# Attention and two mixture-of-experts layers on one core: a small copy moves from ScalarE to VectorE and two range checks move to other places

## The chip, the cores and the metric

The kernel runs on one core of a Trainium2 chip. The metric is the device time of that core in microseconds (us), and the figure compared is the median of the timed runs. The engines are named as the profile names them: PE is TensorE's matmul, PEld its weight load, DVE is VectorE, ACT is ScalarE, POOL is GpSimd, SP is SyncE. In the trace each engine works off its own list of instructions, one behind another, and where it stands idle the row names the engine that released it.

## What is computed

A recurrent attention over 768 steps for 4 batches of 8 heads of width 40, then a router that sends each of the 3072 tokens to one of 8 experts, then a second two-layer net. Cut to what matters here:

```python
def _attn_ref(r, k, v, w, a, b):
    state = np.zeros((B, H, D, D)); y = np.zeros_like(r)
    for t in range(S):
        y[:, :, t] = einsum('bhd,bhde->bhe', rt, state)
        Sa = einsum('bhde,bhe->bhd', state, at)
        state = state * wt[:, :, None, :] - einsum('bhd,bhe->bhde', Sa, bt)
        state = state + einsum('bhd,bhe->bhde', vt, kt)

def reference(...):
    x = attention reshaped to (3072, 320)
    x = moe(x)      # argmax gate, relu(x @ w1[e]) @ w2[e], times the gate
    return moe2(x)  # (max(h,0) + alpha*min(h,0)) @ w_out with h = x @ w_in
```

## The kernel before

The attention handles the time axis in chunks of 64 steps. Its 3072 rows are cut into six groups (two pairs of batches by three stretches of 256 steps); in this document they are group 1 to group 6, in the code `os[0]` to `os[5]`. A group has four chunks for each of two batches, so eight slots, 48 slots in all. A chunk is solved in closed form: the decay products of its steps come from scans, the chunk's triangular matrix is inverted, and what is left is matmuls.

What a group needs before its slots:

- `prepare` (lines 440 to 477), four times a group: three loads, a range check of the decays on ACT (line 466), the backward scan `s` on DVE (467), a reciprocal on DVE (468), the forward scan `q` on DVE (469), two multiplications into `kb` on POOL (472), the copy of the scan's first column into `o.s0` on ACT (473), two multiplications into `abd` on POOL (476).
- `products` (479 to 506) and `sides` (508 to 523), eight times: matmuls into `lp`, copies of the triangular part `l1`, `l2` by ACT (497, 498), one fill of `l2` by POOL (503), the masked product `la` by DVE (504), and transposes whose results ACT evacuates (517, 523).
- `inverse` (528 to 613), once: `ul`, a block transpose of `l2` by DVE (535); then 31 steps of two DVE instructions each that build `ut` (553, 555), with `tmp` and pieces of `ul` in a one-buffer PSUM bank of tag `mg`; then two block transposes of `ut` by DVE, `ttc` (575) and `t11` (578, called `t` in the profile); four POOL copies for each half that put the diagonal blocks into `tt` (571); and for each half a matmul `zp`, ACT copies `z` (603), a matmul `yp`, ACT copies back into `tt` (612). The `zp` of the first half lies in the same `mg` bank as `tmp`.

Two checks of the inverse stand in its second half (589, 590). `check` (431 to 436) squares and sums its source on ACT; it writes the squares to a place that it may spoil, and the sum to one column of `checks`. The check of `ut` spoils `ut` itself, so it has to come after the last reader of `ut`, the transpose `t11`. The check of `l1` spoils `ttc`, so it has to come after the eight POOL copies that read `ttc`. In the timelines of ACT the instructions listed behind a check start only after it.

In the main loop (854 to 884) each slot runs `stage_a` to `stage_e`; DVE's part in a slot is `va` (696), the state update `yc` and `sm` (711, 712) and `rs` (724), POOL's part is `vg` (675), `va` (665), `yt` (725) and, each second slot, two indirect DMAs for the router (971). The inverse of a group is asked for at the first slot of the group before it, and its second half at the first slot of its own.

Only the first prologue is written out by hand as a schedule. After that a scheduler (`schedule_with_timeline_sim=True`) chooses the order on each engine when the program is built, by a timeline of its own, with `issue_after` as a further constraint. So an edit can change the order of instructions that it does not name. The first group (`o.start`) is handled in the prologue and keeps its checks as they are.

Of the kernel before, what the change touches and what calls it, by code (L numbers as in the profile page):

```python
# [9 lines left out]
F32 = mybir.dt.float32  # L10
# [4 lines left out]
AF = mybir.ActivationFunctionType  # L15
# [5 lines left out]
P = 128  # L21
# [269 lines left out]
class Attention:  # L291
# [9 lines left out]
    def __init__(self, tc, ctx, k, wP, kbP, aP, rvP, vrow, rt):  # L301
        nc = self.nc = tc.nc
        self.tc = tc
        self.k = k
        self.wP, self.kbP, self.aP, self.rvP, self.vrow = wP, kbP, aP, rvP, vrow
        st = ctx.enter_context(tc.tile_pool(name="at_st", bufs=1))
        self.early = ExitStack()
        self.pa = self.early.enter_context(tc.tile_pool(name="at_a", bufs=1, side="right"))
        self.p = ctx.enter_context(tc.tile_pool(name="at", bufs=2))
        self.ctx = ctx  # L310
        self.ps = ctx.enter_context(tc.tile_pool(name="at_ps", bufs=1, space=PSUM))
        self.ut_room = ExitStack()
        self.pools = {"ut": self.ut_room.enter_context(tc.tile_pool(name="at_ut", bufs=1, space=PSUM))}
        self.count = {}
        self.region = ExitStack()
        self.region.enter_context(tc.manual_schedule(engines={mybir.EngineType.DVE, mybir.EngineType.Pool, mybir.EngineType.Activation}))

        self.st = st
        V, G = nc.vector, nc.gpsimd
        every = lambda t: t  # L320
        nw = 2 * NCS * CW
        zero = st.tile([P, 1], F32, name="zero")
        nc.vector.memset(zero, 0.0)
        def clear(t):

            nc.scalar.copy(t, zero[:t.shape[0]].to_broadcast(list(t.shape)))

        self.clear = clear
        ring = self.ring
        self.wz = ring("wz", 2, [PP, nw + 1], None, pool=self.pa)  # L330
        self.kb = ring("kb", 2, [P, 2 * NCS, 2, C], None, pool=self.pa)
        self.abd = ring("abd", 2, [P, 2 * NCS, P], None, pool=self.pa)
        V.memset(self.wz[0], 0.9)
        for eng, t in ((V, self.kb[0]), (G, self.kb[1]), (G, self.abd[0]), (G, self.abd[1])):
            eng.memset(t, 0.0)
        self.d1s = ring("d1s", 1, [PP, nw], V, (every, 1e-10), (lambda t: t.rearrange("p (c t) -> p c t", t=CW)[:, :, C:], 1.0), dt=BF16, pool=self.pa)[0]
        self.z = ring("z", 1, [P, 2, 8, C], G, (every, 0.0), pool=self.pa)[0]
        self.d1q = ring("d1q", 1, [PP, nw], V, (every, 0.0), pool=self.pa)[0]
        V.memset(self.wz[1], 0.9)
        self.ra = ring("ra", 2, [PP, 2 * NCS, C], None, pool=self.pa)  # L340
        self.tt = ring("tt", 3, [P, 2, 8, P], None)
        flat = lambda t: t.rearrange("p a b c -> p (a b c)")
        for t in self.tt[:2]:
            self.clear(flat(t))

        self.kb_start = self.kb + [self.tt[0][:, i].rearrange("p u (x t) -> p u x t", x=2) for i in range(2)]
        self.abd_start = self.abd + [self.tt[1][:, i] for i in range(2)]
        self.mid = ring("mid", 1, [P, 1], G, (every, -0.9 * 1.24))[0]
        self.checks = ring("checks", 1, [P, 36], G, (every, 0.0))[0]

        self.negmask = ring("negmask", 1, [P, C], G, (every, -1.0))[0]
        self.posmask = ring("posmask", 1, [P, C], G, (every, 1.0))[0]
        for q in range(2):
            r = slice(q * 64, q * 64 + 64)
            for t, sg in ((self.negmask, 1), (self.posmask, -1)):
                nc.gpsimd.affine_select(t[r], t[r], pattern=[[-sg, C]], compare_op=ALU.is_gt, fill=0.0, base=0, channel_multiplier=sg)
        self.ncheck = 0
        self.rt = rt
# [13 lines left out]
    def ring(self, name, n, shape, eng, *fills, dt=F32, pool=None):  # L372
        pool = pool or self.st
        out = []
        for i in range(n):
            t = pool.tile(shape, dt, name=f"{name}{i}", bufs=1)
            for sel, val in fills:
                eng.memset(sel(t), val)
            out.append(t)
        return out  # L380
# [59 lines left out]
    def prepare(self, o, pg):  # L440

        nc = self.nc
        nw = 2 * NCS * CW
        half, bb = divmod(pg, 2)
        p4 = slice(4 * bb, 4 * bb + 4)
        if pg == 0:
            o.s0 = self.p.tile([PP, 8, NCS], F32, name="s0", bufs=4)
            o.group, o.q, o.la, o.kbr = {}, {}, {}, {}
        if bb == 0:
            o.q[half] = self.p.tile([PP, 8, 2, CW], F32, name="q", bufs=5)  # L450
        kbs, abds = (self.kb_start, self.abd_start) if o.start else (self.kb, self.abd)
        wz, ra, kb, abd = (self.ringed(*n) for n in (("wz", self.wz), ("ra", self.ra), ("kb", kbs), ("abd", abds)))
        for q in range(2):
            r = slice(q * HQ, q * HQ + D)
            nc.sync.dma_start(wz[r], self.wP[o.bp, o.g, pg, q])
            nc.sync.dma_start(kb[r].rearrange("p a x t -> p (a x t)"), self.kbP[o.bp, o.g, pg, q])
            nc.sync.dma_start(ra[r].rearrange("p a t -> p (a t)"), self.aP[o.bp, o.g, pg, q])
        w3 = wz[:, :nw].rearrange("p (c t) -> p c t", t=CW)[:, :, 1:]
        s = self.pa.tile([PP, nw], F32, name="s", bufs=2)
        s3 = s.rearrange("p (c t) -> p c t", t=CW)  # L460
        qt = o.q[half][:, p4]
        qc = qt.rearrange("p a c t -> p (a c) t")
        if o.start:
            self.check(w3, self.pa.tile([P, 2 * NCS, C], F32, name="junk", tag="t4", bufs=3)[:PP], 1.24, self.mid)
        else:
            self.check(w3, qc[:, :, :C], 1.24, self.mid)
        nc.vector.tensor_tensor_scan(s[:, ::-1], wz[:, 1:][:, ::-1], self.d1s[:, ::-1], 0.0, ALU.mult, ALU.max)  # L467
        nc.vector.reciprocal(self.d1q.rearrange("p (c t) -> p c t", t=CW)[:, :, 0], s3[:, :, 0])
        nc.vector.tensor_tensor_scan(qt.rearrange("p a c t -> p (a c t)"), wz[:, :nw], self.d1q, 0.0, ALU.mult, ALU.max)  # L469
        for x in range(2):  # L470
            eng = nc.vector if o.start else nc.gpsimd
            eng.tensor_tensor(kb[:PP, :, x, :], kb[:PP, :, x, :], s3[:, :, 1:], op=ALU.mult)
        nc.scalar.copy(o.s0[:, p4, 2 * half:2 * half + 2], s3[:, :, 0].rearrange("p (a c) -> p a c", c=2))
        for q in range(2):
            r = slice(q * HQ, q * HQ + D)
            nc.gpsimd.tensor_tensor(abd[r, :, q * C:(q + 1) * C], ra[r], qc[r, :, :C], op=ALU.mult)  # L476
        o.group[pg] = abd.rearrange("p (a c) t -> p a c t", c=2), kb.rearrange("p (a c) x t -> p a c (x t)", c=2)
# [50 lines left out]
    def inverse(self, o):  # L528

        nc = self.nc  # L530
# [31 lines left out]
        def vacant(half):  # L562
            if not o.start:
                for lo, hi in zip(lows, highs):
                    nc.gpsimd.memset(o.tt[half][lo, :, :, hi], 0.0)

        def diagonal(half):
            for q in (1, 3, 0, 2):
                r = slice(32 * q, 32 * q + 32)
                eng = nc.vector if o.start and half == 0 else nc.gpsimd  # L570
                eng.tensor_scalar(o.tt[half][r, :, :, 32 * q:32 * q + 32], ttc[r, 2 * half:2 * half + 2], 1.0, 0.0, op0=ALU.mult, op1=ALU.add)

        vacant(0)
        ttc = self.t4("ttc")
        nc.vector.transpose(ttc.rearrange("p c u t -> p t (c u)"), ut)
# [9 lines left out]
        for half in range(2):  # L585
            if half:
                vacant(1)
                diagonal(1)
                self.check(ut, ut, 0.01)
                self.check(l1.rearrange("p c u j -> p (c u) j"), ttc.rearrange("p c u t -> p (c u) t"), 0.01)  # L590
                yield
            tt = o.tt[half]
            zp = self.work("zp", [P, 8, C], "mg" if o.start or half == 0 else "w1")
# [15 lines left out]
                nc.tensor.matmul(yp[c2 * 64:c2 * 64 + w.shape[1], u], lhsT=w, rhs=z[:, c2, u, :], start=True, stop=True)  # L609
            for c2 in range(2):  # L610
                for q, (lo, hi) in enumerate(zip(lows, highs)):
                    nc.scalar.activation(tt[lo, c2, :, hi], out(yp, c2, q), AF.Copy, scale=-1.0)
            yield


# [120 lines left out]
    def run(self, rt, sp, moe, ctx):  # L736
        tc, nc = self.tc, self.nc
        os = []
        for bp in range(B // 2):
            for g in range(S // SL):  # L740
                o = K()
                o.bp, o.g, o.rv, o.start = bp, g, {}, not os
                os.append(o)
        per = 2 * NCS
        n_slots = per * len(os)
# [144 lines left out]
    def bad(self, okm):  # L890

        nc = self.nc
        assert self.ncheck == 36
        ok = self.p.tile([P, 36], F32, name="ok", bufs=1)
        nc.vector.tensor_scalar(ok, self.checks, 1.0, None, op0=ALU.is_le)
        nc.vector.tensor_reduce(okm, ok, axis=AX.X, op=ALU.min)

# [550 lines left out]
```

## Time and profile before

| what | value |
|---|---|
| median of 3 timed runs | 1079.31 us (1078.1 to 1081.4) |
| the profiled execution: its own time | 1070.25 us |
| the profiled execution: its span | 1068.5 us |
| busy in the span: PE, DVE, ACT, POOL | 91%, 64%, 50%, 45% |
| mean granted clock of TensorE | 0.975 |

The profile is one execution, taken by the hardware profiler. Its span runs from the first instruction to the last, and 1.75 us lie around it. In its rows a line such as L436 is the line of the kernel's file; `a<-b` names the tile written and the tile read. In a timeline, the columns are start, duration, engine, line, operation, tiles, shapes and count, and in brackets the idle time of that engine just before and what ended it. The six `ul` transposes, one a group, start at 36.7, 99.4, 164.0, 231.6, 301.4 and 364.7 us, and the last expert work ends the span.

### The profile page before, as it was taken

What the parts mean: (1) busy time and instruction counts of PE and PEld (TensorE: products, weight loads), DVE (VectorE), ACT (ScalarE), POOL (GpSimd) and SP (SyncE); (2) the same over time, 40 slices, a digit from 0 to 9 for tenths busy, and PEclk for the clock granted to TensorE, in tenths of its full rate; (3) what the DMA queues carried; (4) which work ended last, traced back from release to release, by engine and by line L of the source; (5) the groups of instructions that cost most, each with busy time, mean ns of one, the idle gap of its engine ahead of it and who ended that gap; (6) DMA issues with size and microseconds to landing.
All of it is one profiled execution on the core that took longest, in us unless ns stands there. A gap on an engine that the chain in (4) does not pass through costs nothing.

```text
span 1068.5 us, 24465 instructions
## 1 busy us (share of the span) xinstructions
PE 973.1 (91%) x9311; PEld 869.3 (81%) x9311; DVE 683.8 (64%) x1440; ACT 538.6 (50%) x1315; POOL 479.1 (45%) x576
## 2 busy tenths in 40 slices
PE   3658988898899898899999999999999999999997
PEld 2547867777788777788999999978989988988896
DVE  8795978969779695466687776644534454444433
ACT  4647776786677777655566655521312122222211
POOL 7765677786887645320000000034334343435332
PEclk9779999999999999899999999999999999999999
DMA  4362333433333234627787866610000000000000
GB/s 123 95 218 70 77 83 80 104 82 86 89 84 88 49 72 127 159 80 221 222 261 254 262 188 183 186 41 26 25 3 23 26 25 25 26 26 25 25 1 28
DMA packets 126048, 103.34 MB, mean 97 GB/s; under 512 B 90596, under 2 KB 108004, under 8 KB 125924
## 3 DMA queue, kind: packets, MB, share of 16 engines
q1 hardware_dynamic: 122596, 89.90, 29.8%
q0 software_dynamic: 3328, 11.80, 3.5%
q8 instruction: 76, 1.25, 0.5%
q14 instruction: 48, 0.39, 0.1%
HBM read 79.39 MB, written 22.28 MB: 95 GB/s over the span
## 4 chain that ended last, share of the span: by engine, by line
PE 68%; DVE 15%; DMA 5%; issue 4%; ACT 4%; POOL 3%; SPq 0%; POOLq 0%; DVEq 0%; ACTq 0%
PE ph L244 26%; PE po L244 25%; DVE tmp L553 2%; DVE ut L555 2%; PE lp L496 2%; PE pp L651 2%; PE sa L691 2%; PE tr_ps L272 2%; DVE s L467 2%; DVE q L469 2%; DVE va L696 2%; PE yc L707 2%; DMA kb<-in_kbP_dram 2%; PE rvp L662 1%; DMA wz<-in_wP_dram 1%
## 5 line engine op out<-in xcount | busy, mean ns | idle before, releaser
L235 POOL TENSOR_TENSOR gl<-g,gh 128x512 fp32r<-128x512 f32 x96 | 123.9, 1293 | 211.4 <-ACT gh L234 121.1
L234 ACT ACTIVATE gh<-g 128x512 fp32r<-128x512 f32 x96 | 60.7, 632 | 253.3 <-DVE g L1335 186.2
L1334 DVE TENSOR_SCALAR g<-ph,al 128x512 f32<-128x512 f32 x96 | 72.1, 751 | 158.2 <-PE ph L244 74.3
L244 PE MATMUL ph<-x2thi,win 128*128 128x512 f32 x480 | 158.7, 396 | 1.3 <-DVE g L1335 1.3
L244 PE MATMUL po<-wout,gh 128*128 128x320 f32 x768 | 138.8, 309 | 0.0
L244 PEld LDWEIGHTS po<-wout,gh 128*128 128x128 f32 x768 | 121.6, 188 | 5.7
L244 PE MATMUL ph<-x2tlo,win 128*128 128x512 f32 x288 | 114.0, 397 | 0.0
L244 PEld LDWEIGHTS ph<-x2thi,win 128*128 128x128 f32 x480 | 88.6, 188 | 16.3 <-DVE g L1335 1.8
L244 PE MATMUL ph<-xthi,we 128*128 128x448 f32 (+2 forms) x360 | 90.7, 326 | 0.0
L244 PE MATMUL po<-wout,gl 128*128 128x320 f32 x384 | 82.7, 311 | 0.0
L244 PE MATMUL po<-we,hh 128*128 128x320 f32 (+1 forms) x440 | 82.4, 312 | 0.3 <-ACT hh L1153 0.3
L496 PE MATMUL lp<-kb,abd 128*128 128x128 f32 x352 | 59.4, 313 | 24.9 <-POOL abd L476 10.2
L1120 POOL DMA_DIRECT2D xe<-xs_d x16 | 10.1, 634 | 157.8 <-PE tr_ps L272 155.7
L476 POOL TENSOR_TENSOR abd<-ra,q 40x512 f32<-40x512 f32 x44 | 64.7, 1472 | 21.7 <-PE ap L520 13.3
L496 PEld LDWEIGHTS lp<-kb,abd 128*128 128x128 f32 x352 | 50.3, 216 | 29.3 <-POOL abd L476 11.2
L244 PEld LDWEIGHTS po<-we,hh 128*128 128x128 f32 (+1 forms) x440 | 68.0, 180 | 2.8 <-ACT hh L1153 0.5
L244 PE MATMUL ph<-xtlo,we 128*128 128x448 f32 (+2 forms) x216 | 69.9, 325 | 0.0
L1153 ACT ACTIVATE hh<-ph 128x448 fp32r<-128x448 f32 (+2 forms) x70 | 31.9, 457 | 72.7 <-PE ph L244 50.2
L1335 DVE SCALAR_TENSOR_TENSOR g<-ph,g 128x512 f32<-128x512 f32 x96 | 66.3, 691 | 3.1
L244 PEld LDWEIGHTS po<-wout,gl 128*128 128x128 f32 x384 | 63.8, 188 | 2.7
L555 DVE TENSOR_TENSOR ut<-ut,tmp 128x31 f32<-128x31 f32 (+15 forms) x186 | 62.6, 337 | 4.1
L244 PEld LDWEIGHTS ph<-xthi,we 128*128 128x128 f32 x360 | 63.0, 189 | 2.8
(227 smaller groups left out, 2297.4 us busy)
## 6 DMA issues: line engine op xcount, KB each, us to landing
raw<-in_moe_w_dram SPq DMA_DIRECT2D x16, 512.0 KB
raw<-in_moe_w_dram SPq DMA_DIRECT2D x16, 480.0 KB
kb<-in_kbP_dram SPq DMA_DIRECT2D x44, 160.0 KB
r<-in_moe_w_in_dram SPq DMA_DIRECT2D x10, 512.0 KB
r<-in_moe_w_out_dram SPq DMA_DIRECT2D x10, 512.0 KB
xs_d<-tt SPq DMA_DIRECT2D x8, 560.0 KB
raw<-in_moe_w_dram SPq DMA_DIRECT2D x16, 256.0 KB
wz<-in_wP_dram SPq DMA_DIRECT2D x48, 81.4 KB
```

The lines of the kernel that those rows point to most:

```text
L234: nc.scalar.activation(hi, src, AF.Copy)
L235: return lo_eng.tensor_tensor(lo, src, f32(hi), op=ALU.subtract)
L244: return nc.tensor.matmul(out, lhsT=lhsT, rhs=rhs, start=start, stop=stop)
L272: nc.tensor.transpose(ps[:q, t:t + m], rows[:m, t // P, c * P:c * P + q], k.ident[:m, :m])
L467: nc.vector.tensor_tensor_scan(s[:, ::-1], wz[:, 1:][:, ::-1], self.d1s[:, ::-1], 0.0, ALU.mult, ALU.max)
L469: nc.vector.tensor_tensor_scan(qt.rearrange("p a c t -> p (a c t)"), wz[:, :nw], self.d1q, 0.0, ALU.mult, ALU.max)
L476: nc.gpsimd.tensor_tensor(abd[r, :, q * C:(q + 1) * C], ra[r], qc[r, :, :C], op=ALU.mult)
L496: nc.tensor.matmul(lp[:, i], lhsT=abd[:, i, c2, :], rhs=kb[:, i, c2, :], start=True, stop=True)
L555: nc.vector.tensor_tensor(ut[:, j + 1:, :m], ut[:, j + 1:, :m], tv, op=ALU.subtract)
L1153: self.hh_i = nc.scalar.activation(hh[:, :n], ph[:, :n], AF.Relu)
L1334: nc.vector.tensor_scalar(g, ph, 0.0, al[:, f:f + 1], op0=ALU.min, op1=ALU.mult)
L1335: g_i = nc.vector.scalar_tensor_tensor(g, ph, 0.0, g, op0=ALU.max, op1=ALU.add)
```

## The change

Three edits, and the count of check columns that follows from them (36 to 41).

1. The copy of the scan's first column into `o.s0` is done by DVE, between the reciprocal and the forward scan, for groups 3 to 6 (`o.at >= 2`, where `o.at` is the group's number from zero). Groups 1 and 2 keep it on ACT. That is 16 of 24 copies.
2. For groups 2 to 6 the check of `ut` is split in two halves of 512 columns, stands right behind the 31 steps, and writes its squares to the PSUM bank that held `tmp`.
3. For groups 2 to 6 the check of `l1` writes its squares onto `l1` itself, and is issued only after the last of the ACT copies into `tt` of the second half.

```diff
@@ prepare
         nc.vector.reciprocal(self.d1q.rearrange("p (c t) -> p c t", t=CW)[:, :, 0], s3[:, :, 0])
+        if o.at >= 2:
+            nc.vector.tensor_copy(o.s0[:, p4, 2 * half:2 * half + 2], s3[:, :, 0].rearrange("p (a c) -> p a c", c=2))
         nc.vector.tensor_tensor_scan(qt.rearrange("p a c t -> p (a c t)"), wz[:, :nw], self.d1q, 0.0, ALU.mult, ALU.max)
...
-        nc.scalar.copy(o.s0[:, p4, 2 * half:2 * half + 2], s3[:, :, 0].rearrange("p (a c) -> p a c", c=2))
+        if o.at < 2:
+            nc.scalar.copy(o.s0[:, p4, 2 * half:2 * half + 2], s3[:, :, 0].rearrange("p (a c) -> p a c", c=2))
@@ inverse
+        if not o.start:
+            for i in range(2):
+                rows = ut[:, 16 * i:16 * i + 16].rearrange("p a b -> p (a b)")
+                self.check(rows, bank, 0.01)
         vacant(0)
...
-                self.check(ut, ut, 0.01)
-                self.check(l1.rearrange("p c u j -> p (c u) j"), ttc.rearrange("p c u t -> p (c u) t"), 0.01)
+                if o.start:
+                    self.check(ut, ut, 0.01)
+                if o.start:
+                    self.check(l1.rearrange("p c u j -> p (c u) j"), ttc.rearrange("p c u t -> p (c u) t"), 0.01)
...
-                    nc.scalar.activation(tt[lo, c2, :, hi], out(yp, c2, q), AF.Copy, scale=-1.0)
+                    done = nc.scalar.activation(tt[lo, c2, :, hi], out(yp, c2, q), AF.Copy, scale=-1.0)
+            if half and not o.start:
+                with self.tc.issue_after(done.ins):
+                    src = l1.rearrange("p c u j -> p (c u) j")
+                    self.check(src, src, 0.01)
             yield
```

## Rows read from the trace of the kernel before

**Rows 1.** The page, part 1: busy time, share of the span, instructions.
```profile
PE 973.1 (91%) x9311; PEld 869.3 (81%) x9311; DVE 683.8 (64%) x1440; ACT 538.6 (50%) x1315; POOL 479.1 (45%) x576
```

**Rows 2.** Waits, 100 to 450 us: total us, times, longest.
```profile
ACT s L473 <- DVE s L467: 25.3, 13, 2.9
DVE la L504 <- ACT l L498: 22.1, 7, 4.2
...
ACT ut L436 <- DVE t L578: 10.0, 5, 2.5
```

**Rows 3.** Windows of 8 us: PE, PEld, DVE, ACT, POOL busy, clock, DMA.
```profile
136.00:144.00 8.00, 6.63 (x103) 5.41 (x103) 7.69 (x22) 6.21 (x20) 6.88 (x8) 1.00 0.28 61
...
152.00:160.00 8.00, 7.29 (x113) 6.31 (x113) 1.84 (x5) 7.76 (x24) 7.22 (x10) 1.00 0.19 61
```

**Rows 4.** Timeline of DVE: end of group 2's inverse, start of group 3's.
```profile
145.48 1.94 DVE L575 STREAM_TRANSPOSE ttc<-ut 128x1024 f32<-128x1024 f32 x1
...
164.04 2.00 DVE L535 STREAM_TRANSPOSE ul<-l 128x1024 f32<-128x1024 f32 x1 [1.69 <-POOL l L503]
```

**Rows 5.** Timeline of POOL in that gap, first and last of its work.
```profile
147.58 5.38 POOL L571 TENSOR_SCALAR tt<-ttc 32x512 f32<-32x512 f32 x8 [2.05 <-DVE ttc L575]
...
162.70 1.30 POOL L503 TENSOR_SCALAR l<-l 32x512 f32<-32x512 f32 x2
```

**Rows 6.** Groups of instructions by line: busy us, mean ns, idle before.
```profile
L436 ACT ACTIVATE q<-wz,mid 104x512 f32<-104x512 f32 x20 | 14.3, 718 | 5.4 <-DMA wz<-in_wP_dram 3.4 <-POOL yt L725 1.9
...
L436 ACT ACTIVATE ut<-ut 128x1024 f32<-128x1024 f32 x6 | 6.3, 1050 | 12.7 <-DVE t L578 12.7
...
L473 ACT COPY s<-s 104x8 f32<-104x8 f32 x24 | 4.8, 203 | 39.2 <-DVE s L467 39.1
```

**Rows 7.** Timeline of ACT in the gap between groups 2 and 3.
```profile
149.26 1.06 ACT L436 ACTIVATE ut<-ut 128x1024 f32<-128x1024 f32 x1 [2.00 <-DVE t L578]
...
159.17 0.28 ACT L498 COPY l<-lp 128x128 f32<-128x128 f32 x1
```

**Rows 8.** Chain that ended last, 345 to 372 us.
```profile
358.87 1.15 ACT ttc L436 x2
...
368.60 0.21 DVE tmp L553
```

**Rows 9.** Timeline of DVE behind group 6's inverse.
```profile
418.33 0.88 DVE L696 TENSOR_TENSOR va<-sa,posmask 64x256 f32<-64x256 f32 x2 [8.12 <-ACT va L693]
```

**Rows 10.** Chain that ended last, 213 to 234 us: start, us, what.
```profile
222.69 1.05 ACT ttc L436 x2
...
231.62 2.03 DVE ul L535
```

**Rows 11.** Timeline of DVE, gap between groups 4 and 5.
```profile
300.19 1.32 DVE L469 TENSOR_TENSOR_SCAN q<-wz,d1q 104x520 f32<-104x520 f32 x1 [0.65 <-ACT q L436]
```

**Rows 12.** Timeline of POOL, the same gap.
```profile
299.12 1.30 POOL L503 TENSOR_SCALAR l<-l 32x512 f32<-32x512 f32 x2
```

**Rows 13.** Timeline of ACT and of DVE before group 2's inverse.
```profile
97.38 0.20 ACT L473 COPY s<-s 104x8 f32<-104x8 f32 x1 [2.75 <-DVE s L467]
...
99.44 1.98 DVE L535 STREAM_TRANSPOSE ul<-l 128x1024 f32<-128x1024 f32 x1 [0.52 <-POOL l L503]
```

**Rows 14.** Chain that ended last, 125 to 180 us: the reciprocal on DVE.
```profile
136.71 0.12 DVE d1q L468
```

**Rows 15.** Timeline of DVE: two backward scans, two tiny instructions of the router.
```profile
134.74 1.24 DVE L467 TENSOR_TENSOR_SCAN s<-wz,d1s 104x520 f32<-104x520 f32 x1
...
151.05 0.58 DVE L969 TENSOR_SCALAR slot_i<-sl 128x2 int32<-128x2 f32 x1
...
185.93 0.20 DVE L969 TENSOR_SCALAR slot_i<-sl 128x2 int32<-128x2 f32 x1
...
208.54 2.20 DVE L467 TENSOR_TENSOR_SCAN s<-wz,d1s 104x520 f32<-104x520 f32 x1
```

**Rows 16.** Timeline of POOL beside the last of those scans.
```profile
208.46 3.26 POOL L476 TENSOR_TENSOR abd<-ra,q 40x512 f32<-40x512 f32 x2
```

More of the change, by code (lines that the diff above doesn't have):

```diff
@@ L348, in __init__ @@
         self.mid = ring("mid", 1, [P, 1], G, (every, -0.9 * 1.24))[0]
-        self.checks = ring("checks", 1, [P, 36], G, (every, 0.0))[0]
+        self.checks = ring("checks", 1, [P, 41], G, (every, 0.0))[0]
         self.negmask = ring("negmask", 1, [P, C], G, (every, -1.0))[0]
@@ L741, in run @@
                 o = K()
-                o.bp, o.g, o.rv, o.start = bp, g, {}, not os
+                o.bp, o.g, o.rv, o.start, o.at = bp, g, {}, not os, len(os)
                 os.append(o)
@@ L892, in bad @@
         nc = self.nc
-        assert self.ncheck == 36
-        ok = self.p.tile([P, 36], F32, name="ok", bufs=1)
+        assert self.ncheck == 41
+        ok = self.p.tile([P, 41], F32, name="ok", bufs=1)
         nc.vector.tensor_scalar(ok, self.checks, 1.0, None, op0=ALU.is_le)
```

## The prediction, made before the changed kernel ran

> **What bounds the kernel now.** Over the whole span PE is the busiest engine [rows 1], but the change touches only the attention, so its own stretch has to be read. The table of waits for 100 to 450 us comes first: ACT stands 25.3 us for the scan `s` in front of the copy into `s0`, and 10.0 us for the transpose `t11` in front of the check of `ut`; DVE in turn stands 22.1 us for ACT's copies of `l` [rows 2]. Whether ACT's waits cost anything depends on who sets the pace. The windows show two kinds of stretch that alternate. In 136 to 144 us DVE is busy 7.69 of 8 us; in 152 to 160 us DVE falls to 1.84 while ACT has 7.76 and POOL 7.22 [rows 3]. The first kind is the 31 steps of an inverse: DVE sets the pace, and an ACT that waits for DVE loses nothing. The second kind is the gap from the end of one inverse, `ttc` at 145.48, to the start of the next, `ul` at 164.04: 18.6 us [rows 4]. Four such gaps exist (between groups 2 and 3, 3 and 4, 4 and 5, 5 and 6), and a tail behind group 6. The change can gain only in the gaps and in the prologue; on DVE it can lose anywhere in the inverses.
>
> Within the first gap POOL goes from the diagonal copies at 147.58 to the fill of `l2`, which ends at 164.00 and releases `ul` [rows 4, 5], nearly without a pause: 7.22 of 8 us in the middle [rows 3]. ACT is as full. So the gap has two limits that lie close together, and relief for ACT alone may stop at POOL.
>
> **Part by part.**
>
> *Check of `ut`.* It goes from one instruction of 1.05 us to two of 512 columns; the nearest row is the decay check of 512 columns, 0.72 us [rows 6]. That is 1.44 instead of 1.05, and 0.4 us more ACT work a group. Writing to PSUM is shown by no check here; between nothing more and half of 1.05 each I take 0.72, the row of the same length. What it wins is its place. Before, ACT waited for `t11` until 149.26 with 2.00 us idle [rows 7]; the new check needs only the last of the 31 steps, before `ttc` at 145.48 [rows 4], so it can run while DVE does both transposes (1.94 us each) and cover itself there. If that cover is gone, it holds up everything behind it on ACT (`va`, `l`, `z`) by up to 1.44 us.
>
> *Check of L.* Some 1.05 us, 1.15 with its sum [rows 8], leave the middle of the gap and stand behind the second `tt` copies. In groups 2 to 5 these fall into the next inverse, where ACT has slack. In group 6 there is no next inverse: DVE waits 8.12 us for ACT's `va` right behind those copies [rows 9], so there the 1.15 us return on the same path, and I count nothing for group 6 (between +1.15 and -1.15).
>
> *What this gives gap by gap.* Groups 2/3: by the present order POOL alone sets the end, gain 0. But `l2`'s fill stands behind other POOL work although ACT delivered `l` at 159.45 and the fill started at 162.70 [rows 5, 7]; the scheduler may bring it forward, by at most 3.25 us. I take a third, 1.1. Groups 3/4: the check of L lies on the chain that leads to `ul` with 1.05 us [rows 10]. If POOL is as full here as in the first gap, 0; if not, up to 2.2 (1.05 for each check and the sums); I take 1.5, as here the chain names ACT and not POOL. Groups 4/5: `ul` starts behind a scan `q` that had waited for ACT's decay check until 300.19, and the scan kept DVE for another 1.3 us [rows 11], while POOL's fill had ended at 300.42 [rows 12]; so 1.0 is there, 0 if the scan keeps its lead and its wait. Groups 5/6: the check of L stands on the chain with 1.15 us, and the first step of the next inverse follows at 368.60 [rows 8]; I take 1.0 (0 to 1.15). Sum 4.6, between 0 and 7.6.
>
> *Copy into `s0`.* ACT loses 16 copies of 0.20 us and the waits in front of them [rows 6]. Inside the inverses this is worth nothing. In the prologue it is worth something: ACT waited 2.75 us for the third of group 3's copies, and group 2's `ul` then waited 0.52 us for POOL's fill, which had waited for ACT's `l` [rows 13]. I take 0.5 (0 to 0.5). DVE gains 16 instructions of the reciprocal's size (104x8). On the chain a reciprocal takes 0.12 us [rows 14]; 13 copies lie in stretches where DVE sets the pace, so 1.6 us. The other bound is what a tiny DVE instruction costs when POOL is in the middle of something: `slot_i` took 0.20 us once and 0.58 another time, and the same scan 1.24 and 2.20 us, the longer one beside two `abd` products of 1.6 us each [rows 15, 16]. If the copy has to sit out the rest of such a product, half of 1.6 us, 0.8, comes on top. Of the 12 scans of groups 4 to 6, two of which stand in rows 15, six ran 1.9 us or more, so that would be 4.8 us. I take none of it, since the copy may be placed among other DVE work, and keep it for a rival.
> The Trainium skill, page "SBUF — State Buffer", section "Who interferes with whom", speaks against this edit: a VectorE copy that uses both port pairs and a GpSimd instruction exclude each other, and the second to start waits until the first is done. The two durations of `slot_i` and of the scan fit that, though no row here shows a DVE copy from SBUF to SBUF. By the rule the edit costs those 4.8 us more, by the reciprocal's row not.
>
> *The queues passed.* No DMA moves. `checks` grows from 36 to 41 columns; its one comparison at the end costs nothing that a row could show. `l1` is held longer (until behind the second `tt` copies), but its two buffers are needed again a group later, more than 40 us.
>
> *Sum.* 4.6 + 0.5 - 1.6 = 3.5 us less. For the profiled execution: 1070.25 - 3.5 = 1066.8. Its time lies 9.1 us under the median of the runs, so the forecast for the median is 1079.31 - 3.5 = 1075.8.
>
> **The rivals.**
>
> *Nothing moves (the relief stops at POOL).* The scheduler leaves POOL's order, the fills stay where they are, the stall on ACT is exchanged for another. Then 0 for the first two gaps, 1.0 and 1.0 for the others, 0.5 in the prologue, less 1.6: 0.9 us gained, 1078.4. For it: in the first gap POOL has no pause [rows 5]. Against it: the chain of the second gap names ACT's check, not POOL [rows 10]. It is also the case in which the edit doesn't do what it says, since the file's order is not the engine's order.
>
> *Slower: the copies wait for POOL.* Place: DVE inside the inverses of groups 2 to 5, where nothing hides them. Price: 1.6 + 4.8 against the 2.5 of the former rival: 3.9 us more, 1083.2. It decides from about half of the exposed copies on: above 2.5 - 1.6 = 0.9 us of such waits the kernel is slower, above some 4 us by more than can be told apart. For it: the scan's 2.20 beside `abd`. Against it: the reciprocal, of the same shape and from the same tile, shows 0.12 right behind a scan [rows 14].
>
> *Slower: `zp` waits for the check.* The new check writes to the `mg` bank that `zp` of the first half needs. If ACT comes to it only after other copies, `zp` starts late. ACT was idle for 2.00 us before 149.26 [rows 7], and two checks of 0.72 [rows 6] with 0.1 each for the sums need 1.6, so the cover is thin: 0.4 us. A check that comes 1 us later in each of five groups, with the gains of the last two gaps gone, costs 5 x 0.6 + 1.6 - 0.5 = 4.1 us, 1083.4.
>
> **How the numbers follow.** About 0.3%, 3.2 us, is what a measurement of this kernel can tell from no change. Forecast (some order of POOL's or DVE's queue uses ACT's relief, 3.2 us or more gained): 0.47. Nothing moves: 0.27. Copies wait for POOL: 0.17. `zp` waits: 0.09. So faster 0.47, same 0.27, slower 0.26. The range: the upper bounds of all gains, 7.6 + 0.5, plus 1.15 in group 6 give 9.3 us, and the scheduler may carry a pair of `abd` products (3.26 us) past a fill once: 1079.3 - 12.5 = 1066.8, taken as 1067. Above, the two slower cases stand at 1083.2 and 1083.4; with 1.6 for a group 6 in which the moved check costs its 1.15 and one `abd` wait of half a us, 1085.
>
> **What would show it.** Right: the wait of ACT's check for `t11` and ACT's wait in front of `s0` are gone from the table; the four gaps from `ttc` to `ul` are shorter by 1 us or so each; DVE's copies take about 0.2 us. Wrong: the gaps keep 18 us or more with POOL without a pause; DVE's copies show 0.6 us and more and the inverses from `ul` to `ttc` become longer; or `zp` of the first half waits for ACT. A large gain or loss outside the gaps and inverses, from a new order of the queues, is what these steps cannot see.

## The result, and the profile after

The changed kernel takes 1083.22 us in the median (1077.56 to 1088.93) against 1078.24 us (1071.44 to 1082.36) for the kernel before beside it: a ratio of 1.0058, 95% interval 1.0034 to 1.0082 (estimated from all executions; the two medians alone give 1.0046, 5.0 us). It is slower; the prediction, 1075.8 us and faster, had the wrong sign.

The two profiled executions are extremes (1070.25 us before is 1.2 us under the fastest of the eight, 1088.93 after is the slowest), so their difference of 18.7 us overstates the change. Executions of one kernel spread over some 14 us here, and much of that goes with TensorE's clock: among 35 executions of the kernel before on one chip, one hundredth of mean granted clock (0.952 to 0.975) goes with 5.3 us. Single profiles are therefore used below for stretches and rows, and only the ratios for the time.

What the first two edits did can be read from the page and the groups by line of the changed kernel (columns as in [rows 6]):

```profile
PE 981.3 (90%) x9311; PEld 874.4 (80%) x9311; DVE 685.9 (63%) x1456; ACT 538.8 (50%) x1309; POOL 479.6 (44%) x576
```
```profile
L436 ACT ACTIVATE tmp<-ut 128x512 f32<-128x512 f32 x10 | 6.0, 600 | 5.7 <-DVE ut L558 5.6
...
L470 DVE COPY s<-s 104x8 f32<-104x8 f32 x16 | 5.6, 349 | 0.1
```

The half checks of `ut` take 0.60 us, not 0.72 as estimated from [rows 6], and ScalarE's waits for the scan and for `t11` [rows 2] are gone between 100 and 450 us. The second wait was exchanged for half of it: the half checks now wait 5.6 us for the last of the 31 steps. And the 16 copies on VectorE take 0.35 us in the mean, where the sum had 0.12 [rows 14].

The gap between groups 2 and 3, VectorE's timeline (beside [rows 4]):

```profile
147.38 1.96 DVE L582 STREAM_TRANSPOSE ttc<-ut 128x1024 f32<-128x1024 f32 x1
...
161.84 0.42 DVE L507 TENSOR_TENSOR la<-lp,negmask 128x256 f32<-128x256 f32 x1 [4.05 <-ACT l L501]
165.94 0.88 DVE L709 TENSOR_TENSOR va<-sa,posmask 64x256 f32<-64x256 f32 x2 [3.68 <-ACT va L706]
166.85 1.24 DVE L471 TENSOR_TENSOR_SCAN q<-wz,d1q 104x520 f32<-104x520 f32 x1
168.01 1.99 DVE L538 STREAM_TRANSPOSE ul<-l 128x1024 f32<-128x1024 f32 x1
```

and GpSimd's in the same gap (beside [rows 5]):

```profile
163.35 1.30 POOL L506 TENSOR_SCALAR l<-l 32x512 f32<-32x512 f32 x2
```

The fill of `l2` did come forward, from 17.22 us behind `ttc` (162.70 - 145.48) to 15.97 (163.35 - 147.38). That is 1.25 us, close to the 1.1 of the prediction. It brought nothing: `ul` could have started at 164.65, but in VectorE's new list a slot's `va`, which waits 3.68 us, and a scan `q` of 1.24 us stand in front of it. The gap became 20.63 us instead of 18.56. TensorE ran out of work in it, 1.76 us before 149.94, where the `kbr` copy on ScalarE ends the wait; the second half of the new check stands right in front of that copy:

```profile
148.63 0.59 ACT L436 ACTIVATE tmp<-ut 128x512 f32<-128x512 f32 x1
149.23 0.20 ACT L436 ACTIVATION_READ_ACCUMULATOR tmp<-ut 128x1 f32 x1
149.46 0.43 ACT L520 COPY kbr<-bp 128x320 f32<-128x320 f32 x1
```
```profile
149.94 0.58 PE L523 MATMUL ap<-ident,abd 104*128 104x104 f32 x4 [1.76 <-ACT kbr L520]
```

TensorE's clock fell after it. The windows of the changed kernel, columns as in [rows 3]:

```profile
144.00:152.00 8.00, 5.06 (x82) 4.25 (x82) 7.87 (x21) 4.32 (x14) 5.38 (x10) 0.98 0.34 85
152.00:156.00 4.00, 4.00 (x25) 3.21 (x24) 1.12 (x3) 1.88 (x6) 3.55 (x6) 0.50 0.03 6
```

A granted clock of 0.50 is 1.2 GHz; the kernel before had 1.00, 2.4 GHz, in both windows of its gap. That the idle time brought the clock down is not shown: the kernel before has TensorE idle for 2.15 us before 148.93, and its clock stayed at 1.00. Nor does the new check alone explain it: the kernel before in the changed kernel's order, without that check (before_as_after, below), shows 0.61 from 152 to 156 us.

### The profile page after: what moved, and what is told of

Same layout as the page of the kernel before. It is cut to its first block, busy times and chain, and to the rows that moved or that the text cites. A ratio compares the mean times of both kernels' runs of the same rounds, so it can differ in the third digit from the quotient of the medians.

```text
span 1087.1 us, 24464 instructions
## 1 busy us (share of the span) xinstructions
PE 981.3 (90%) x9311; PEld 874.4 (80%) x9311; DVE 685.9 (63%) x1456; ACT 538.8 (50%) x1309; POOL 479.6 (44%) x576
## 3 DMA queue, kind: packets, MB, share of 16 engines
q8 instruction: 76, 1.25, 0.5%
## 4 chain that ended last, share of the span: by engine, by line
PE 66%; DVE 13%; DMA 7%; POOL 5%; ACT 5%; issue 4%; SPq 0%; POOLq 0%; DVEq 0%; ACTq 0%
PE ph L244 25%; PE po L244 24%; PE lp L499 3%; PE tr_ps L272 2%; DMA raw<-in_moe_w_dram 2%; DVE q L471 2%; PE yc L720 2%; DVE s L467 2%; PE sa L704 2%; PE pp L664 2%; DVE tmp L556 1%; DVE ut L558 1%; PE rvp L675 1%; POOL kb L474 1%; PE ap L523 1%
## 5 line engine op out<-in xcount | busy, mean ns | idle before, releaser
L479 POOL TENSOR_TENSOR abd<-ra,q 40x512 f32<-40x512 f32 x44 | 62.3, 1416 | 22.5 <-PE ap L523 12.5
```

## The experiments

Three theories were put against each other. **Theory 1:** the copies on VectorE wait for GpSimd (the prediction's rival). **Theory 2:** the checks in their new places hold up ScalarE or `zp`. **Theory 3:** the edits make the scheduler list all engines' work anew, and the loss is in the lists.

### The parts alone, the scheduler left free

`a_only` is edit 1 of the diff above alone, `b_only` edit 2, `c_only` edit 3, `bc` edits 2 and 3.

```diff
# a_only
+        if o.at >= 2:
+            nc.vector.tensor_copy(o.s0[...], s3[:, :, 0]...)
# b_only
+                self.check(rows, bank, 0.01)
-                self.check(ut, ut, 0.01)
# c_only
+                with self.tc.issue_after(done.ins):
+                    self.check(src, src, 0.01)
-                self.check(l1..., ttc..., 0.01)
```

> The first edit alone: the copy into s0 on DVE for groups 3 to 6, both checks as before. Theory 1 (the copies wait for POOL; in the changed kernel's trace 16 of them took 5.6 us, 0.12 us the shortest and 0.94 the longest): slower by 3 to 5 us, that is all of the loss. Theory 2 (the checks are at fault: the first half of the inverse's zp waits for them, and ACT's list is held up): same within 1.5 us. Theory 3 (any edit makes the scheduler list the engines' work anew, and the loss is in those lists, in TensorE's idle times and its falls to 1.2 GHz): anything between -5 and +6 us, with the gaps between inverses changed by whole microseconds though no check was moved.

> The second edit alone: the check of ut in two halves to PSUM behind the 31 steps. Theory 1: same or up to 2 us faster. Theory 2: slower by 3 to 6 us, zp of the first half starts later behind the POOL copies than before, and ACT waits for the last of the 31 steps with other copies behind it. Theory 3: any sign, with new lists.

> The third edit alone: the check of L in place behind the copies into T. Theory 1 and theory 2: faster by 1 to 3 us, since 1.15 us leave ACT's list in four gaps and nothing else moves. Theory 3: any sign.

> Both checks moved, the copy into s0 left on ACT. Theory 1: faster by 1 to 4 us. Theory 2: slower by 2 to 5 us. Theory 3: not the sum of the two edits alone.

| kernel | ratio to before | interval |
|---|---|---|
| a_only | 1.0078 | 1.0049 to 1.0106 |
| b_only | 1.0018 | 0.9995 to 1.0042 |
| c_only | 1.0057 | 1.0032 to 1.0083 |
| bc | 1.0052 | 1.0025 to 1.0079 |

The parts do not add up to 1.0058, and a_only alone, 8.4 us, lost more than any theory had allowed it. And c_only, which only takes 1.06 us of ScalarE's time out of each gap, is slower by 0.57%, where theories 1 and 2 had it faster by 1 to 3 us. Its VectorE timeline in the gap between groups 4 and 5 shows one place:

```profile
304.05 0.42 DVE L504 TENSOR_TENSOR la<-lp,negmask 128x256 f32<-128x256 f32 x1 [5.79 <-PE rvp L667]
305.72 1.50 DVE L469 TENSOR_TENSOR_SCAN q<-wz,d1q 104x520 f32<-104x520 f32 x1 [1.25 <-ACT q L436]
307.25 0.21 DVE L468 RECIPROCAL d1q<-s 104x8 f32<-104x8 f32 x1
307.56 1.84 DVE L469 TENSOR_TENSOR_SCAN q<-wz,d1q 104x520 f32<-104x520 f32 x1
309.44 0.88 DVE L701 TENSOR_TENSOR va<-sa,posmask 64x256 f32<-64x256 f32 x2
310.35 2.01 DVE L535 STREAM_TRANSPOSE ul<-l 128x1024 f32<-128x1024 f32 x1
```

Two scans and a reciprocal of a later `prepare` run while `ul` waits its turn: GpSimd's fill had ended at 305.41. The kernel before had one scan there [rows 11].

### The order held

To part an edit from the order that it brings, each engine's list was held: for any two neighbours in a given kernel's list an edge of order only was added, with no wait on the chip. Instructions that the given kernel doesn't have (moved checks, copies on the other engine) are placed by the scheduler between the held ones.

```diff
     with _tile.TileContext(nc, schedule_with_timeline_sim=True) as tc:
         the_kernel(tc, *args)
+        ins = list(tc.nc.cur_bb.bb.instructions)
+        for row in ORDER:  # one row an engine: the other kernel's list
+            for a, b in zip(row, row[1:]):
+                tc.add_manual_dep(ins[b], ins[a].name, edge)
```

`after_held`, `a_held`, `b_held`, `c_held` and `bc_held` are the change and its parts in the order of the kernel before. `before_as_after` and `before_as_c` are the kernel before, without any edit, in the order of the changed kernel and of c_only. `before_again` is the kernel before, once more.

> The whole change, but every instruction that the kernel before has too is held in its place in the kernel before's order on all five engines (edges of order only, no added waits); only the 16 copies of the first column and the 15 moved checks are placed anew. Theory 1 (the change itself costs time: the copies of the first column wait for GpSimd, 16 x 0.23 us = 3.7 us of excess in the changed kernel's trace): still slower than the kernel before by 3 to 6 us, a ratio of 1.003 to 1.006. Theory 3 (the loss lies in the new order that the scheduler gave to all the other instructions): the loss goes away; with the gaps' gain of up to 4.6 us less the copies' 3.7 us the ratio is 0.997 to 1.001.

> The kernel before without any of the change, but all instructions that it shares with the changed kernel held in the changed kernel's order on all five engines; only its own copies of the first column on ACT and its own checks are placed by the scheduler. Theory 3 (the order is what costs): slower than the kernel before by 3 to 8 us, a ratio of 1.003 to 1.008, with nothing of the change in it. Theory 1 (the edits are what costs): within 0.2% of the kernel before.

> The check of L moved behind T's copies, alone, everything else held in the kernel before's order. With the order free this part alone took 1.0057. Theory 3: the loss goes away and what is left is the bare worth of 1.06 us of ScalarE's time taken from each gap: a ratio of 0.996 to 1.000. Theory 2 (the check in its new place holds up the copies that follow it on ScalarE): still 1.004 to 1.007.

> The first column's copy on VectorE from the third group on, alone, everything else held in the kernel before's order. With the order free this part alone took 1.0078. Theory 1 (contention): 16 copies of 0.35 us each, 5.6 us, of which some half lies on VectorE's chain, a ratio of 1.002 to 1.005. Theory 3: the order is the larger part, and a ratio of 1.000 to 1.003 is left; both theories meet here between, so what counts is how much of 0.0078 goes away: under a third by theory 1, over half by theory 3.

> The check of ut to PSUM as soon as it is made, alone, everything else held in the kernel before's order. If the three parts add up at that order (whole 1.0058, copies 1.0046, check of L 0.9988), this one is at 1.0024: theory 2, the check in two halves delays what stands behind it on ScalarE. If it is hidden as the prediction put it, 0.998 to 1.001.

> Both checks as the change has them, the first column's copy left on ScalarE, everything else held in the kernel before's order. With the order free this took 1.0052. Theory 3 (order) with harmless checks: 0.997 to 1.001. Theory 2 (the checks cost in their new places): 1.002 to 1.005.

> The kernel before once more, as a measure of what two executions of one program differ by: ratio 1.000 within its interval of some 0.0028, and a second profile with another share of TensorE's clock, in which the five stretches from the end of one inverse to the start of the next are read again. If they stay at 18.56, 18.35, 19.85 and 17.93 us within 0.5 us or so, the stretches of 20.6 to 26.4 us in the kernels with a new order are due to the order; if they scatter by 2 us and more, they are not.

> The kernel before, its check of L where it was, but everything that it shares with the kernel of the moved check of L held in that kernel's order. Order theory: 1.004 to 1.008, as slow as that kernel (1.0057), with nothing of the change in it. Rival (the place of the check is what costs): 0.998 to 1.001.

| edit | order free | held in the order of before |
|---|---|---|
| none | 0.9996 (0.9966 to 1.0027) | the same |
| copies | 1.0078 (1.0049 to 1.0106) | 1.0046 (1.0018 to 1.0074) |
| check of `ut` | 1.0018 (0.9995 to 1.0042) | 0.9994 (0.9968 to 1.0019) |
| check of L | 1.0057 (1.0032 to 1.0083) | 0.9988 (0.9959 to 1.0016) |
| both checks | 1.0052 (1.0025 to 1.0079) | 1.0000 (0.9971 to 1.0028) |
| all | 1.0058 (1.0034 to 1.0082) | 1.0058 (1.0034 to 1.0083) |

| no edit, in the order of | ratio |
|---|---|
| the changed kernel | 1.0055 (1.0026 to 1.0084) |
| c_only | 1.0036 (1.0010 to 1.0061) |

Theory 3 holds for the checks: in the old order they cost nothing that can be told (which also says that holding an order costs nothing by itself), and the new orders without them cost, within the intervals, as much as with them (before_as_c, at 1.0036, fell just under the 1.004 forecast). As an account of the time theory 2 falls. But after_held refutes theory 3 as the whole story: in the old order the change is just as slow, by the copies. How much of their loss is order a_held does not say: 41% of the 0.0078 went away, between the third and the half that would have decided, and a second measurement of the same kernel, below, gave 1.0076. Two losses, then, either of them large enough alone. They do not add up in the changed kernel; why not, these runs don't show.

The second profile of the kernel before (before_again) came out against the use of single gaps. Three of its four gaps are within 0.3 us of the first profile's, but the one between groups 3 and 4 took 20.61 us instead of 18.35, with the same program. By the rule set before that run, stretches of 20.6 us and more do not show an order by themselves. Only the gap between groups 2 and 3 is steady enough: 18.53 to 18.61 us in all ten profiles in the old order, and 20.63 and 20.68 in the two in the changed kernel's order, of which the second, before_as_after, has no edit.

And the checks gained nothing either. The reason is in the gap between groups 3 and 4, where the chain had named the check of L [rows 10]. The end of that gap in GpSimd's timeline, the kernel before and then bc_held, from which both checks are gone:

```profile
229.55 0.69 POOL L725 TENSOR_TENSOR yt<-rs,q 104x256 f32<-104x256 f32 x1
230.18 0.16 POOL L369 MEMSET ut<- 128x32 f32 x1
230.27 1.30 POOL L503 TENSOR_SCALAR l<-l 32x512 f32<-32x512 f32 x2
```
```profile
233.98 0.69 POOL L735 TENSOR_TENSOR yt<-rs,q 104x256 f32<-104x256 f32 x1
234.61 0.17 POOL L369 MEMSET ut<- 128x32 f32 x1
234.70 1.30 POOL L503 TENSOR_SCALAR l<-l 32x512 f32<-32x512 f32 x2
```

In the kernel before the fill ended at 231.57, and `ul` started at 231.62: GpSimd's chain was as late as the one through the check. In bc_held `ul` starts at 236.04, and the chain that ended last now names GpSimd:

```profile
233.98 0.69 POOL yt L735
234.67 0.10 POOL ut L369
234.78 0.55 POOL l L503
235.32 0.07 issue
235.39 0.62 POOL l L503
236.01 0.02 issue
236.04 2.03 DVE ul L535
```

From `ttc` to the fill it is 17.00 us before (230.27 - 213.27) and 16.97 after (234.70 - 217.73); the gap is 18.35 and 18.31.

The other two gaps show no gain either. Between groups 4 and 5 the three kernels with held checks have 20.01 to 22.26 us against 19.85, and in c_held the scan `q` in front of `ul` still waits 0.59 us for ScalarE's decay check, as in [rows 11]; between groups 5 and 6 they have 18.12 to 18.34 against 17.93.

### Copy or reduction

In `a_red_held` each of the 16 copies is replaced, in the same place of the same list, by a reduction over one element, which gives the same values.

```diff
-            nc.vector.tensor_copy(o.s0[...], s3[:, :, 0]...)
+            nc.vector.tensor_reduce(o.s0[...], s3[:, :, 0:1]..., axis=AX.X, op=ALU.max)
```

> The first column's copy on VectorE from the third group on, held in the kernel before's order as in the run that took 1.0046, each of the 16 copies in exactly the same place, but written as a maximum over an axis of one element, which gives the same values with an operation that is no copy. Theory 1 (it is the wait for GpSimd that costs): the 16 take 0.12 to 0.20 us each without the ones of 0.8 to 0.97 us, 2 to 3 us in all instead of 6.6, and the ratio falls to 1.000 to 1.002. Rival (the cost lies in having any instruction there, on VectorE's chain, or in the order): the durations may fall, but the ratio stays at 1.003 to 1.006.

It took 1.0033 (1.0006 to 1.0061): in the rival's range, but with intervals this wide that tells neither theory from the other. Copies and reductions were therefore run side by side on one chip (`a_held_2`, `a_red_held_2`, the same two kernels).

> The first column's copies on VectorE, all else held in the kernel before's order, a second time, beside the same kernel with reductions. As before 1.0046, within 1.002 to 1.007. Theory 1 (the wait for GpSimd is most of the cost): above the reductions by 0.003 or so, 16 x 0.28 us = 4.5 us of VectorE's time less.

> The reductions in the copies' places, a second time. Theory 1: 1.000 to 1.002, since 2.1 us of VectorE's time are left, and 1.4 of them on its chain. Rival (most of the cost is something else than the copies' waits, such as the later start of the forward scan or ScalarE's changed pace): 1.003 to 1.005, less than 0.0015 under the copies.

Copies: 1.0076 (1.0048 to 1.0103). Reductions: 1.0014 (0.9984 to 1.0044). Side by side the intervals do not meet, and the reductions are 0.62% or 6.7 us faster; in the first pair, on two chips, it was 0.13% or 1.4 us. Over both the means are 1.0061 and 1.0024, 0.37% or 4.0 us apart. The two kernels' rows by source line (least, median and largest ns; a_held, then a_red_held):

```profile
L470 DVE COPY s<-s x16: 118/174/971, 85.7 to 328.7; 104x8 f32<-104x8 f32 x16
```
```profile
L470 DVE TENSOR_REDUCE s<-s x16: 111/119/168, 84.2 to 325.1; 104x8 f32<-104x8 f32 x16
```

One copy, VectorE and GpSimd in a_held:

```profile
148.43 0.27 DVE L556 TENSOR_TENSOR tmp<-tmp,ut 128x135 f32<-128x135 f32 x1
148.62 0.89 DVE L470 COPY s<-s 104x8 f32<-104x8 f32 x1
149.42 0.28 DVE L558 TENSOR_TENSOR ut<-ut,tmp 128x135 f32<-128x135 f32 x1
```
```profile
146.22 3.25 POOL L479 TENSOR_TENSOR abd<-ra,q 40x512 f32<-40x512 f32 x2
```

and the same place in a_red_held:

```profile
147.06 0.15 DVE L470 TENSOR_REDUCE s<-s 104x8 f32<-104x8 f32 x1
147.19 0.30 DVE L558 TENSOR_TENSOR ut<-ut,tmp 128x135 f32<-128x135 f32 x1
```
```profile
144.66 3.26 POOL L479 TENSOR_TENSOR abd<-ra,q 40x512 f32<-40x512 f32 x2
```

The copy ends at 149.51, the two `abd` products at 149.47; the reduction runs in the middle of them in 0.15 us. Every copy of a_held that took over 0.2 us ends so, within 0.1 us behind a GpSimd instruction. In a_held the 16 copies take 6.6 us in all, the reductions 2.1. So the wait for GpSimd is 4.5 us. That copies cost time which reductions in their place do not is shown by the run side by side; that most of the 4.5 us lies on the path fits the mean of 4.0 us, but with pairs of 1.4 and 6.7 us its size is not shown. Theory 1 holds for the copies in kind. What the reductions themselves cost (0.24% in the mean of two runs) is not told either: one interval holds 1, the other does not.

### Whose list costs

Three kernels took c_only and held one engine's list as in the kernel before, the others free.

> The check of L moved behind T's copies, alone; only VectorE's order is held as in the kernel before, the other four engines are listed by the scheduler. With all orders free 1.0057, with all held 0.9988. If the loss lies in VectorE's list (scans of a later prepare and a va that waits stand in front of the next group's ul), most of it goes away here: 0.998 to 1.002. If it lies in ScalarE's or TensorE's list: 1.004 to 1.007.

> The same with only ScalarE's order held. If the loss lies in VectorE's list: 1.004 to 1.007, as VectorE is listed anew here. If it lies in ScalarE's list: 0.998 to 1.002.

> The same with only TensorE's order held. If the loss lies in VectorE's list: 1.004 to 1.007. If it lies in TensorE's list: 0.998 to 1.002.

| held | ratio | sum of the four gaps, us |
|---|---|---|
| none (c_only) | 1.0057 (1.0032 to 1.0083) | 83.8 |
| ACT | 1.0089 (1.0054 to 1.0124) | 79.3 |
| DVE | 1.0041 (1.0012 to 1.0069) | 74.9 |
| PE | 1.0020 (0.9992 to 1.0048) | 75.9 |
| all (c_held) | 0.9988 (0.9959 to 1.0016) | 75.1 |

The guess that VectorE's list carries the loss is not borne out by the time: with it held 0.998 to 1.002 was expected, and 0.4% is lost, although the gaps of that profile are as short as before. Its stretch behind group 6's `ttc` takes 669.8 us (1078.6 - 408.8), against 663.4 to 668.1 in the profiles with all lists held; whether the loss lies there one profile can't say. Holding ScalarE's list alone cures nothing (1.0089, from six executions). TensorE's comes nearest, but its interval doesn't part it from VectorE's. Which list it is stays open.

Sums over the profiles, from the starts of `ttc` and `ul` in VectorE's timelines: the four gaps come to 74.7 to 77.6 us in every kernel in the old order (ten profiles, mean 76.4), and to 78.8 to 83.8 where VectorE's and TensorE's lists are both new (eight, mean 80.9), with or without an edit in it. The five inverses of groups 2 to 6 come to 225.7 to 234.6 us without the copies on VectorE (mean 230.3), and to 233.2 to 240.0 with them (mean 236.7); the two kernels with reductions lie at 235.2 and 234.1, so these sums don't separate the wait from the mere presence as the times do. So the means put the order's cost in the gaps, some 4.5 us, and the copies' in the inverses, some 6 us. For the order that place is not shown: the grouping was made after the runs, b_only has 83.0 us of gaps at a ratio of 1.0018, and c_hold_dve 74.9 at 1.0041. Nor are gaps and inverses all: of the 18.6 us between the two profiled spans 6.5 lie behind group 6's `ttc` (672.7 against 666.2 us, the longest of all profiles). No kernel tried here is faster than the kernel before by more than can be told.

## Why the prediction was wrong

*What bounds the kernel* was right: VectorE sets the pace in the inverses and can only lose there, and in the gaps GpSimd's limit lies close behind ScalarE's.

*The step that failed first is the price of the copy.* I took 0.12 us from a reciprocal of the same shape [rows 14], which is only the piece of it that the chain counts: that instruction took 0.20 us, and it stood behind a step of the inverse, not behind a scan. The 24 reciprocals took 0.15 to 0.21 us, none longer. I kept the other bound, half an `abd` product, for a rival at 0.17. The nearer rows were those of other forms: the scan of 1.24 and 2.20 us beside `abd` and the `slot_i` of 0.20 and 0.58 [rows 15, 16]. Same shape was not same behaviour: the reduction, also of that shape, takes 0.13 us, the copy up to 0.97. The rival priced this at 4.8 us on top of 1.6; measured were 4.5 of wait in the old order and 3.7 in the changed kernel (5.6 - 16 x 0.12). There only three of the ten copies over 0.2 us sat out an `abd` product; the others ended with GpSimd's fills, copies and products of other tiles. The rival's total of 1083.2 us agrees with the median of 1083.22, but by luck in part: it counted 2.5 us of gains that did not come, it had no price for the new order, and the kernel before beside it took 1078.24 and not the 1079.31 that it started from. The rule of the Trainium skill that the prediction cited (page "SBUF — State Buffer", section "Who interferes with whom") agrees with the trace: the copy ends with GpSimd's instruction, 149.51 against 149.47. The same section of the Trainium skill has an instruction with one SBUF input outside the two-port modes stay clear of GpSimd; the reductions agree, at 0.17 us at most.

*The checks' gain of 4.6 us was not there.* The sum gave 1.5 us to the gap between groups 3 and 4, since "the chain names ACT and not POOL". A chain names only the last of the limits. The fill that ended at 231.57, 0.05 us ahead of `ul`, was in GpSimd's timeline and not looked up; it alone makes the gain 0. In the old order the gaps of b_held, c_held and bc_held are 18.53 to 18.59 us between groups 2 and 3, against 18.56. The 0.5 us of the prologue did not show either: group 2's `ul` starts at 99.75 in the changed kernel, 99.44 and 99.79 in the two profiles of the kernel before. And group 6, counted as nothing, costs something: with the check of L in front of it, VectorE's `va` starts 18.27 us behind `ttc` instead of 16.00, and its wait is 9.40 us instead of 8.12; over all profiles it starts 15.99 to 17.14 us behind `ttc` where the check stayed in its place, and 16.67 to 18.49 where it moved.

*The rival in which `zp` waits for the check* is not borne out in the time: the same checks cost nothing in the old order, 0.9994. In the gap between groups 2 and 3 `zp` starts 3.46 us behind `ttc` in the changed kernel, 3.45 before. But between groups 4 and 5 something like it is there: in b_held and bc_held `zp` starts 7.31 and 7.16 us behind `ttc`, against 5.57 before and 5.61 in c_held. A half check stands in front of `kbr` on ScalarE, TensorE waits 1.24 us for that copy, and in bc_held its granted clock is 0.50 in the 3 us after 291. The row of `zp` shows no wait of its own, so what delays it stands before it in TensorE's list, and is not the bank; a_red_held, without a moved check, has 6.88, so part of the delay may be scatter. The half checks were shorter than feared (0.60 us), though ScalarE did put other copies between the two halves.

*The new lists* were named at the very end as what these steps cannot see, with no price. That was the second step that failed: the changed kernel's order costs 0.55% by itself, as much as the whole change. The range, 1067 to 1085 us, held the time only thanks to the two slower rivals.

## What to carry to other kernels

Where a scheduler lists the work anew after each edit, an edit is timed together with a new order; hold the old order and the edit's own worth shows, put the new order on the old kernel and the order's does. Before counting a gain on a chain, look up when the second input of its last instruction was ready: unless that input comes earlier too, the gain is at most that distance, here 0.05 us. And a tiny instruction on the engine that sets the pace is priced by its operation and by what runs beside it, not by its shape.

## What the runs showed of the hardware

A VectorE copy of 104x8 took 0.12 us at the least and up to 0.97 beside a GpSimd product of 2.0 us, ending with it; a reduction of the same data in the same place took 0.11 to 0.17. A squared sum of 512 columns on ScalarE took 0.60 us from SBUF to PSUM, and 0.72 in another check, of 104 partitions, that wrote to SBUF. One program's 35 executions on one chip spread by 1.3% (1070.8 to 1084.5 us), and their mean granted clock went with it (0.952 to 0.975, correlation -0.82). In the twenty profiles, of different kernels, TensorE's granted clock in the stretch up to group 2's `ul` is 0.69 to 0.85, and the stretch takes 99.4 to 99.8 us in the three at 0.83 and 0.85, and 102.2 to 104.6 in the seven at 0.69 and 0.70.
